# Two MLP groups of a fused attention and MLP layer go from 16 to 18 paired rows in seven products; one maximum for two tiles, a mask by GpSimd, and a few moved instructions

## The chip, the cores and the metric

The kernel runs on one core of a Trainium2 chip. The core has five engines that run their own instruction streams: TensorE (PE in the profile, with its weight loads listed apart as PEld), VectorE (DVE), ScalarE (ACT), GpSimd (POOL) and SyncE (SP), which here only issues DMAs. Semaphores order them. The metric is the device time of one execution in microseconds, the median over runs.

## The reference

One transformer layer over 2048 positions of width 576, in bfloat16, without learned norms:

```python
x = A_x
h = x + A(_layernorm(x))          # 32 heads of 18; key s-2w for w in 0..7, softmax over 8 logits, then @ wo
h2 = h + B(_layernorm(h))         # gelu(y @ w1 + b1) @ w2 + b2, inner width 4608
```

In the attention each position looks at itself and at seven earlier positions, two apart; positions before the start are masked with -1e9.

## The kernel before

**Tiles and groups.** The 2048 positions are 16 tiles of 128 rows, `x3[:, j, :]`. Row p of tile j is position 16p + j, so the keys "two apart" of one tile lie in the tiles of the same parity, or in the same tiles one row up; only row 0 has masked keys. `ATT_ORDER` is 14, 12, ..., 0, 15, 13, ..., 1, and `GROUPS` are its eight pairs, from (14, 12) to (3, 1). A first stage (to about 65 us) makes Q, K and V for all tiles. Then comes a loop over the eight groups (L1031); its turn for group k is called step k here. `x_all` and `q_all` are the SBUF homes of x and of q, one row of 576 bfloat16 for each tile; rows whose tile is through are used again for other things.

**What a step does.** Step k computes the MLP of group k while VectorE prepares the attention of groups k+1 and k+2. On TensorE a step is: the first MLP product with `w1` (`mlp1`, the tile `pm`), the attention's output product with `wo` for the two tiles c, d of group k+1 (`wo_visit`, `pw`), then the second MLP product with `w2` (`po`). The order of all engines' instructions is written out by hand: lists of hooks (`m1`, `x["hc"]`, `x["h"]`, `x["6"]`, `x["7"]`, `x["in"]`, `x["exp"]`, `x["4"]`, `x["3"]`) are called between the parts of TensorE's work, and each engine runs its share in that order.

**The attention chain.** In step k VectorE makes, for c and d, the weighted sums over V (`pv_sum`: L401, L407, L408, at the start of the step). `send_o` stores the result o to a DRAM scratch `td`, and `read_o` reads it back with a transposing DMA into `oT`, the weights of the `wo` product. After that, still on VectorE: products of q and k for tile e of group k+2 (`att_qk_a`, `att_qk_b`), with a memset that masks row 0 (L364); later the same for f. `att_max` takes the maximum over the 8 keys and subtracts it (L368, L369), ScalarE takes one exponential for both tiles (`exps`), `att_den` divides. The product for f waits by hand for the `pow` on GpSimd that makes the second 1/std of the next norm (`root`, L346).

**The second MLP product in seven products.** `w2` has 36 row blocks; two neighbours make a pair, so there are `NM = 18` pairs. For a pair, two tiles and two halves of the 576 columns make a 2x2 by 2x2 block product. It can be done as eight products, or as seven with sums (Winograd's form): `w2_sums` prepares sums of weights once (four of them, `t_slot`), and `h_sums` in each step prepares four sums of the hidden activations (`s_slot`), which VectorE writes. Groups 0 and 1 use the plain form (`mlp2`); groups 2 to 5 use seven products over the first 16 pairs and the plain form for the last two (`plain`, hooks "11", "12", "21", "22"); groups 6 and 7 (`FULL`) use seven products over all 18. `mlp2_fast` lists the order; "b", "d" and "f" are copies on ScalarE of one PSUM bank to another (L774), which the next product adds to. In step 7 the second product (2) stands after the sixth.

**Homes of the sums.** The four sums of pairs 0 to 11 lie in `kv_ring0` and in `h_all` in place; those of pairs 12 to 15 in rows of `q_all` (15, 13, 11; in step 2 also `x_all` 10 and 8). The weight sums of pairs 16 and 17 are made in step 6 into `kv_ring1`, which is free by then.

**DMA order.** All loads and stores of SP stand in one hand-written queue. The x rows of the odd tiles are loaded a second time (`reload_x`): those of group k+3 late in step k, for k from 1 to 4 (at hook "in" in steps 3 and 4, at "3" in step 2). GpSimd issues the adding DMAs (`out_sum`, `accumulate_h`). The four quarters of `wo` are loaded in the first stage after visits 5 (two), 8 and 11.

Of the kernel before, what the change touches and what calls it, by code (L numbers as in the profile page):

```python
# [17 lines left out]
def kernel(  # L18
# [336 lines left out]

    ADDS = ((0, 0, 9), (0, 0, 4), (0, 0, 2), (0, 0, 1))

    def att_qk_b(j, i, skip=0):
        side[j] = i
        out = logit_of([j])[:, 0]  # L360
        att_qk_add(j, ADDS[skip:])
        nc.vector.tensor_tensor(out=out, in0=prod[:, :, 0:H], in1=prod[:, :, 8 * H:9 * H], op=ALU.add)
        if j // 2 + 1 < W:
            nc.vector.memset(out[0:1, j // 2 + 1:W, :], -1e9)  # L364

    def att_max(js):
        n, sl, lg = len(js), sides(js), logit_of(js)
# [248 lines left out]
    def t_slot(t, m0, m1):  # L616
        if t == 2:
            return w2_block(0, 1, m0, m1).bitcast(F16)
        i = (0, 1, None, 2)[t]
        if m0 >= 16:  # L620
            return ring_blocks(1, (2 * i + m0 - 16) * HALF, m1 - m0, HALF)
        if i == 2 and m0 < 16:
            return ring_blocks(0, RING_T + m0 * HALF, m1 - m0, HALF)
        part = 0 if m1 <= 8 else 1 if m1 <= 12 else 2
        rows, j0 = ((x_all, (1, 9, 13)[part]), (q_all, (4, 12, 0)[part]))[i]
        m = m0 - (0, 8, 12)[part]
        j = j0 + 2 * (m // 2)
# [6 lines left out]
    step_of = [0]  # L634
    RING_T = 3 * SR * P

    def s_slot(t, m0, m1):
        if t == 2:
            return h_block(0, 1, m0, m1)
        i = (0, 1, None, 2)[t]  # L640
        if m0 < SR:
            return ring_blocks(0, (i * SR + m0) * P, m1 - m0, P)
        if not ring1_free[0]:
            rows, j = ((q_all, 15), (x_all, 10), (x_all, 8))[i] if step_of[0] == 2 else (q_all, 15 - 2 * i)
            return rows[:, j, (m0 - SR) * P:(m1 - SR) * P].bitcast(F16).rearrange("p (m c) -> p m c", c=P)
        return ring_blocks(1, 6 * HALF + (i * (NM - SR) + m0 - SR) * P, m1 - m0, P)

    def h_block(odd, i, m0, m1):
        return h_all[:, 2 * m0 + odd:2 * m1:2, i * P:(i + 1) * P].bitcast(F16)
# [53 lines left out]
        return ap.rearrange("p (g c) -> p g c", g=2)  # L703

    def mlp2_fast(g, rows, tags, wo, hooks):
        last, summed = wo is None, rows < NM
# [24 lines left out]

        def out1():
            if summed:
                add(o1[:, HALF:D], bank[5], o1[:, 0:HALF])
                add(o1[:, 0:HALF], b, o1[:, 0:HALF])
                out_sum(j1)
                return
            add(o1[:, 0:HALF], b, rest[:, 0])
            add(o1[:, HALF:D], bank[5], rest[:, 1])
            nc.sync.dma_start(out=out3[:, j1, :], in_=o1)  # L740

        def do_rest():
# [16 lines left out]
        if rows < NM:  # L759
            steps = ["wo", "hc", (1, all_), "b", "h", "e", (7, lo), (2, all_), (6, all_), "6", "7", "d", "11", (7, hi), "rest", "in",  # L760
                      (5, all_), "f", "exp", (4, all_), "21", "22", "o1", "4", (3, all_), "12", "o0", "3"]
        elif not last:
            steps = ["wo", "hc", (1, all_), "b", "h", "e", (7, lo), (6, all_), "6", "d", "7", (2, all_), (7, hi), "rest", "in",
                     (5, all_), "f", (4, all_), "o1", "4", (3, all_), "o0"]
        else:
            steps = ["e", (1, lo), (7, lo), (1, hi), "b", "h", (7, hi), "rest", (6, all_), "d", (2, all_), "lo",
                     (5, all_), "f", (4, all_), "o1", (3, all_), "o0"]
        for step in steps:
            if isinstance(step, tuple):
                product(step[0], bank[step[0]], *step[1])  # L770
            elif step == "f" and last:
                add(f, bank[5], x_of(j0)[:, HALF:D])
            elif step in seed:
                nc.scalar.copy(out=bank[seed[step][1]], in_=bank[seed[step][0]])  # L774
            else:
                call([does[step]] if step in does else hooks.get(step, ()))
# [22 lines left out]
    with tc.manual_schedule(engines={ENG.PE, ENG.Activation, ENG.DVE, ENG.SP, ENG.Pool}):  # L799
# [129 lines left out]
            ln2_ins(c, d)  # L929

        loads = {}
        for v, fns in ((2, [(load_w1, 0)]), (3, [(load_w1, 1)]), (4, [(load_w1, 2)]), (5, [(load_wo, [0, 1])]), (8, [(load_wo, [2])]),
                       (11, [(load_wo, [3])]), (14, [(load_w1, 4)]), (18, [(load_w1, 5), (load_w2, 0)]), (19, [(load_w2, 1)]),
                       (20, [(load_w2, 2)]), (21, [(load_w2, 3)]), (22, [(load_w2, 4)])):
            loads[v] = [c_(*fn) for fn in fns]
        after = {
# [9 lines left out]
                c_(store_halo, A[1]), c_(store_halo, A[0], slice(1, 2))],  # L946
            9: [c_(ln1_act, 9, 0)],
            10: [c_(att_pv, A[0]), c_(ln1_act, 9, 1), c_(in_x, 1), c_(halo, A[1], 1)],
            11: [c_(out_x, 2), c_(halo, A[0], 2)],
            12: [c_(ln1_act, 10, 0)],  # L950
            13: [c_(ln1_act, 10, 1), c_(in_x, 2), c_(out_x, 3), c_(load_w1, 3), c_(store_halo, A[2]), c_(store_halo, A[3])],
            14: [c_(att_pv, A[1]), c_(in_x, 3), c_(load, b2_bc, B_b2.partition_broadcast(P))],
# [71 lines left out]
        def wo_visit(*duos, fill=False):  # L1024
            visit([wo_duo(j, tag) for j, tag in duos], (lambda: [ahead[0]() for _ in range(2)]) if fill else None)

        FULL = (6, 7)
        p, q, r, s = "ABDC"

        gelu_table()  # L1030
        for k, g in enumerate(GROUPS):  # L1031
# [36 lines left out]
            step_of[0] = k  # L1068
            x = {n: [] for n in ("hc", "h", "6", "7", "in", "exp", "4", "3")}
            if 2 < k < 7:  # L1070
                m1[0] += [c_(pv_sum, c), c_(send_o, c), c_(pv_sum, d), c_(read_o, c), c_(send_o, d), c_(read_o, d)]
            if k < 6:
                m1[1] = m1.get(1, []) + [c_(att_qk_a, e), c_(att_qk_b, e, 0)]
                x["hc"] += [c_(halo, e, 1)]
                m1.setdefault(3, [])
                if k == 2:
                    m1[0] += [c_(pv_sum, d), c_(send_o, d), c_(read_o, d)]
# [4 lines left out]
                x["h"] += [c_(h_sums, 0, SR, (1, 3) if k == 2 else (3,)), c_(h_sums, SR, 16)]  # L1082
                x["7"] += [c_(att_max, [e]), c_(att_qk_one, f, 1), c_(att_max, [f])]
                x["exp"] += [c_(exps, e, f)]
                x["4"] += [c_(att_den, e, f)]
            else:
                if k == 6:
                    ring1_free[0] = True
                    m1[1].append(c_(w2_sums, 16, NM))
                m1[3] = m1.get(3, []) + [c_(h_sums, 0, SR)]  # L1090
                if k == 7:
                    mid[3] = {1: [c_(h_sums, SR, 16)]}
                    x["h"] += [c_(h_sums, 16, NM)]
            if k + 3 < len(GROUPS):
# [55 lines left out]
```

## Time and profile before

| | us |
|---|---|
| median of 3 runs (lowest, highest) | 358.68 (357.99, 359.8) |
| the profiled execution, its own time | 358.89 |
| its span, first to last instruction | 357.1 |
| TensorE busy in the span | 352.1 (99%) |
| VectorE busy | 298.1 (83%) |
| ScalarE busy | 235.5 (66%) |
| GpSimd busy | 48.4 (14%) |
| granted TensorE clock | 1.000 |

The page gives busy time by engine, the span in 40 slices, the DMA queues, the chain of work that ended last, and the costliest groups of instructions. Beside it stand answers of the trace: the timeline of one engine (start, duration, engine, line, operation, out<-in, count, and in brackets idle time before it with what ended it), the chain in order of time, and the instructions of one tile with the time from a DMA's issue to its landing. Line numbers are those of the kernel before. Step 3 runs from 177 to 213 us, step 4 to 249, step 5 to 285, step 6 to 320, step 7 to the end.

### The profile page before, as it was taken

What the parts mean: (1) busy time and instruction counts of PE and PEld (TensorE: products, weight loads), DVE (VectorE), ACT (ScalarE), POOL (GpSimd) and SP (SyncE); (2) the same over time, 40 slices, a digit from 0 to 9 for tenths busy, and PEclk for the clock granted to TensorE, in tenths of its full rate; (3) what the DMA queues carried; (4) which work ended last, traced back from release to release, by engine and by line L of the source; (5) the groups of instructions that cost most, each with busy time, mean ns of one, the idle gap of its engine ahead of it and who ended that gap; (6) DMA issues with size and microseconds to landing.
All of it is one profiled execution on the core that took longest, in us unless ns stands there. A gap on an engine that the chain in (4) does not pass through costs nothing.

```text
span 357.1 us, 11588 instructions
## 1 busy us (share of the span) xinstructions
PE 352.1 (99%) x4945; PEld 290.2 (81%) x4945; DVE 298.1 (83%) x428; ACT 235.5 (66%) x524; POOL 48.4 (14%) x63
## 2 busy tenths in 40 slices
PE   8999999999999999999999999999999999999996
PEld 4777878998788877887788778877887788778874
DVE  4999999999988999999999989998999897520431
ACT  4889756996647783668566856695669566706620
POOL 2241004000212010201200220022002200210000
PEclk9999999999999999999999999999999999999999
DMA  7996599953837573742653445345555353262001
GB/s 242 330 317 165 156 262 286 388 200 81 213 71 113 172 230 70 139 72 61 93 97 84 114 106 81 86 107 109 85 86 103 63 88 50 59 126 41 4 1 33
DMA packets 63492, 46.29 MB, mean 130 GB/s; under 512 B 32192, under 2 KB 61760, under 8 KB 63440
## 3 DMA queue, kind: packets, MB, share of 16 engines
q1 hardware_dynamic: 59472, 41.50, 43.7%
q0 software_dynamic: 3744, 3.84, 9.8%
q8 instruction: 38, 0.62, 0.7%
q10 hardware_dynamic: 224, 0.22, 0.2%
q14 instruction: 14, 0.11, 0.1%
HBM read 23.38 MB, written 12.42 MB: 100 GB/s over the span
## 4 chain that ended last, share of the span: by engine, by line
PE 92%; DMA 3%; DVE 2%; ACT 1%; issue 0%; POOL 0%; SPq 0%; ACTq 0%; POOLq 0%
PE pm L222 39%; PE po L687 25%; PE pq L222 12%; PE po L597 10%; PE pw L222 5%; DMA x_all<-in_A_x_dram 1%; DMA wq_sb<-in_A_wqkv_dram 1%; ACT h_all L578 1%; DVE ln_stats L148 1%; DVE q_all L844 0%; DVE kv_ring L667 0%; DVE ln_mv L149 0%; POOL ln_rstd L161 0%; ACT q_all L314 0%; SPq L104 0%
## 5 line engine op out<-in xcount | busy, mean ns | idle before, releaser
L222 PE MATMUL pm<-hnT,w_sb 64*128 64x256 bf16 x2304 | 142.9, 269 | 0.0
L578 ACT ACTIVATE h_all<-pm,b_sb 128x256 f16<-128x256 f32 (+1 forms) x288 | 108.4, 495 | 50.9 <-PE pm L222 50.3
L222 PEld LDWEIGHTS <-w_sb 64*128 64x128 bf16 x2304 | 113.3, 94 | 13.4 <-issue 1.7
L222 PE MATMUL pq<-wq_sb,xnT 64*128 64x288 bf16 x720 | 54.7, 283 | 0.7 <-ACT q_all L314 0.3
L687 PEld LDWEIGHTS <-h_all 128*128 128x128 f16 x464 | 44.8, 98 | 12.9 <-issue 1.4
L222 PEld LDWEIGHTS <-xnT 64*128 64x128 bf16 x864 | 42.0, 94 | 11.7 <-issue 0.8
L353 DVE TENSOR_TENSOR prod<-prod 128x2304 bf16<-128x2304 bf16 (+1 forms) x64 | 44.2, 691 | 2.1
L401 DVE TENSOR_TENSOR prod<-kv_ring,probs 128x4608 bf16<-128x4608 bf16 x16 | 40.9, 2558 | 1.7 <-DMA kv_ring<-kv_dram 1.2
L344 DVE TENSOR_TENSOR prod<-kv_ring,q_all 128x4608 bf16<-128x4608 bf16 x16 | 40.9, 2556 | 1.6 <-POOL ln_rstd L492 1.3
L222 PE MATMUL pm<-hnT,w1h_sb 64*128 64x256 bf16 x288 | 39.5, 269 | 0.0
L407 DVE TENSOR_TENSOR prod<-prod 128x2304 bf16<-128x2304 bf16 (+1 forms) x32 | 33.9, 1058 | 1.1
L597 PEld LDWEIGHTS <-h_all 128*128 128x128 bf16 x288 | 27.8, 98 | 8.0 <-issue 1.2
L687 PE MATMUL po<-w2a_sb,h_all 128*128 128x288 bf16 (+1 forms) x252 | 34.0, 286 | 0.0
L687 PEld LDWEIGHTS <-kv_ring 128*128 128x128 f16 x252 | 24.7, 98 | 6.2
L597 PE MATMUL po<-w2a_sb,h_all 128*128 128x288 bf16 x224 | 28.6, 286 | 0.0
L787 POOL DMA_DIRECT2D x_all<-o_sb x12 | 10.7, 889 | 126.0 <-PE pw L222 72.6
L222 PE MATMUL pq<-wqh_sb,xnT 64*128 64x288 bf16 x144 | 27.4, 283 | 0.0
L492 POOL TENSOR_TENSOR ln_rstd<-ln_var,mhalf 128x1 f32<-128x1 f32 x13 | 10.6, 818 | 77.1 <-ACT ln_var L491 50.1
L667 DVE TENSOR_TENSOR kv_ring<-h_all 128x1536 f16<-128x1536 f16 (+3 forms) x9 | 6.8, 754 | 15.9 <-ACT h_all L578 15.9
L222 PE MATMUL pw<-wo_sb,oT 64*128 64x288 bf16 x256 | 19.5, 283 | 0.0
L161 POOL TENSOR_TENSOR ln_rstd<-ln_veps,mhalf 128x1 f32<-128x1 f32 (+2 forms) x14 | 13.1, 948 | 45.2 <-DVE ln_nmean L481 27.5
L687 PE MATMUL po<-w2b_sb,h_all 128*128 128x288 bf16 (+1 forms) x112 | 18.8, 286 | 0.1
(121 smaller groups left out, 410.9 us busy)
## 6 DMA issues: line engine op xcount, KB each, us to landing
w_sb<-in_B_w_dram SPq DMA_DIRECT2D x6, 768.0 KB, 6.6
kv_ring<-kv_dram SPq DMA_DIRECT2D x28, 144.0 KB, 2.4
kv_dram<-kv_ring SPq DMA_DIRECT2D x13, 288.0 KB, 3.2
w2a_sb<-in_B_w_dram SPq DMA_DIRECT2D x3, 1008.0 KB, 10.0
x_all<-in_B_b_dram SPq DMA_DIRECT2D x15, 144.0 KB, 4.2
td<-q_all SPq DMA_DIRECT2D x14, 144.0 KB, 1.8
td<-hn SPq DMA_DIRECT2D x14, 144.0 KB, 1.8
x_all<-h POOLq DMA_DIRECT2D x14, 144.0 KB, 4.7
```

The source lines that it names most:

```text
L161: nc.gpsimd.tensor_tensor(out=rstd[:], in0=veps[:], in1=mhalf[:].to_broadcast([P, n]), op=ALU.pow)
L222: last = nc.tensor.matmul(duo["g"][r ^ swap][i], lhsT=lhsT, rhs=rhs, start=(swap == 0 and i == 0 and kt == 0), stop=(swap == 1 and kt == K ...
L344: ins = nc.vector.tensor_tensor(out=prod[:], in0=k_ring[j % 2], in1=q_all[:, j, :].unsqueeze(1) .to_broadcast([P, W, D]), op=ALU.mult).ins
L353: nc.vector.tensor_tensor(out=prod[:, :, o * H:o * H + n], in0=prod[:, :, a * H:a * H + n], in1=prod[:, :, c * H:c * H + n], op=ALU.add)
L401: nc.vector.tensor_tensor(out=prod[:].rearrange("p w (d h) -> p w d h", h=H), in0=v_ring[j % 2].rearrange("p w (d h) -> p w d h", h=H), in ...
L407: nc.vector.tensor_tensor(out=prod[:, 0:n, :], in0=prod[:, 0:n, :], in1=prod[:, n:2 * n, :], op=ALU.add)
L492: ins = nc.gpsimd.tensor_tensor(out=rstd[:], in0=var[:], in1=mhalf[:], op=ALU.pow).ins
L578: pace[0] = nc.scalar.activation(out=hT(grp)[:, f, 0:N], in_=ps[:, r, i * N:(i + 1) * N], func=ACT.Gelu_apprx_tanh, bias=b1_sb[:, f:f + 1] ...
L597: nc.tensor.matmul(banks[half], lhsT=hT(grp)[:, f, i * P:(i + 1) * P], rhs=w2_rows(f)[:, half * HALF:(half + 1) * HALF], start=(f == 0), s ...
L667: nc.vector.tensor_tensor(out=s_slot(t, m0, m1), in0=a, in1=b, op=alu)
L687: nc.tensor.matmul(bank, lhsT=l, rhs=r, start=start, stop=stop, skip_group_check=True)
L787: nc.gpsimd.dma_start(out=x_of(j), in_=o_of.pop(j), accum_op=ALU.add)
```

## The change

- `FULL` becomes groups 4 to 7: in steps 4 and 5 all 18 pairs go through the seven products, the plain matmuls go. `summed`, which decides how the outputs are written, is tied to the group instead (groups 6 and 7 differ as before).
- VectorE makes the four activation sums of pairs 16 and 17 in steps 4 and 5. In step 4 it also makes two of the four weight sums of these pairs, in step 3 the other two; step 6 no longer makes them. They lie in `q_all` 15, 13 and 11.
- The homes of pairs 12 to 17 are listed by step (`homes`); in steps 4 and 5 the second sum lies in a tile of tag `hnT`, the buffer of the normed and transposed h (`new_top`). As written, the third home of these steps takes the fourth sum of pairs 12 to 15, then over the same 512 columns the first and the fourth sum of pairs 16 and 17, before the products read them; the values of that part of the output follow from it.
- In steps 4 and 5 the mask of tile e is written by GpSimd between its two `pow`, and the maximum of e and f is taken in one instruction after f's product (one subtraction too). The mask of f stays on VectorE.
- `reload_x` of group k+1 stands in steps 4 and 5 between `send_o(c)` and `read_o(c)`; that of group 7 stays in step 4 at "in"; those in steps 2 and 3 go.
- Step 7: the second product's first six pairs stand between the two parts of the seventh product's last six pairs.
- `wo`: one quarter after visit 5, one after visit 8, and two after visit 11's `out_x`, ahead of the halo read.

```diff
-    def att_qk_b(j, i, skip=0):
+    def att_mask(j, engine=nc.vector):
+        if j // 2 + 1 < W:
+            engine.memset(logit_of([j])[0:1, 0, j // 2 + 1:W, :], -1e9)
+
+    def att_qk_b(j, i, skip=0, mask=True):
...
         if m0 >= 16:
-            return ring_blocks(1, (2 * i + m0 - 16) * HALF, m1 - m0, HALF)
+            return q_all[:, 15 - 2 * i, (m0 - 16) * HALF:(m1 - 16) * HALF].bitcast(F16).rearrange("p (m c) -> p m c", c=HALF)
...
+    homes = {2: ((q_all, 15), (x_all, 10), (x_all, 8)), 3: ((q_all, 11), (x_all, 10), (x_all, 8)),
+             4: ((q_all, 9), (x_all, 4), (x_all, 6)), 5: ((q_all, 9), (q_all, 5), (q_all, 7))}
...
+            if step_of[0] in FULL and t == 1:
+                rows, c = top[0][:].rearrange("p k c -> p (k c)"), 0
+            else:
+                rows, j = homes[step_of[0]][2 if m0 >= 16 else i]
+                rows, c = rows[:, j, :], (16 - SR - i) * P if m0 >= 16 else 0
+            return rows[:, (m0 - SR) * P - c:(m1 - SR) * P - c].bitcast(F16).rearrange("p (m c) -> p m c", c=P)
...
+    def new_top():
+        top[0] = sb.tile([P, KT, 2 * P], BF16, tag="hnT", name="hnT")
...
-            steps = ["e", (1, lo), (7, lo), (1, hi), "b", "h", (7, hi), "rest", (6, all_), "d", (2, all_), "lo",
+            steps = ["e", (1, lo), (7, lo), (1, hi), "b", "h", (7, (SR, 16)), (2, (0, 6)), (7, (16, rows)), "rest", (6, all_), "d",
+                     (2, (6, rows)), "lo",
...
-            11: [c_(out_x, 2), c_(halo, A[0], 2)],
+            11: [c_(out_x, 2), c_(load_wo, [2, 3]), c_(halo, A[0], 2)],
...
-        FULL = (6, 7)
+        FULL = (4, 5, 6, 7)
...
-                m1[0] += [c_(pv_sum, c), c_(send_o, c), c_(pv_sum, d), c_(read_o, c), c_(send_o, d), c_(read_o, d)]
+                m1[0] += [c_(pv_sum, c), c_(send_o, c)] + [c_(reload_x, GROUPS[k + 1])] * (k in (4, 5)) + [c_(pv_sum, d), c_(read_o, c), c_(send_o, d), c_(read_o, d)]
...
-                m1[1] = m1.get(1, []) + [c_(att_qk_a, e), c_(att_qk_b, e, 0)]
-                x["hc"] += [c_(halo, e, 1)]
+                m1[1] = m1.get(1, []) + [c_(att_qk_a, e), c_(att_qk_b, e, 0, 0, k < 4)]
+                x["hc"] += [c_(halo, e, 1)] + [c_(att_mask, e, nc.gpsimd)] * (k >= 4)
...
+                if k in FULL:
+                    x["h"] += [new_top, c_(h_sums, SR, 16), c_(h_sums, 16, NM)] + [c_(w2_sums, 16, NM, (2, 3))] * (k == FULL[0])
...
-                x["7"] += [c_(att_max, [e]), c_(att_qk_one, f, 1), c_(att_max, [f])]
+                first = [e] if k < 4 else []
+                x["7"] += [c_(att_max, first)] * len(first) + [c_(att_qk_one, f, 1), c_(att_max, [f] if first else (e, f))]
+                if k == 3:
+                    x["exp"] += [c_(w2_sums, 16, NM, (0, 1))]
...
-                    m1[1].append(c_(w2_sums, 16, NM))
...
-            if k + 3 < len(GROUPS):
-                x["3" if k == 2 else "in"] += [c_(reload_x, GROUPS[k + 3])]
+            if k == 4:
+                x["in"] += [c_(reload_x, GROUPS[7])]
```

More of the change, by code (lines that the diff above doesn't have):

```diff
@@ L362, in att_qk_b @@
         nc.vector.tensor_tensor(out=out, in0=prod[:, :, 0:H], in1=prod[:, :, 8 * H:9 * H], op=ALU.add)
-        if j // 2 + 1 < W:
-            nc.vector.memset(out[0:1, j // 2 + 1:W, :], -1e9)
+        if mask:
+            att_mask(j)
     def att_max(js):
@@ L633 @@
     ring1_free = [False]
-    step_of = [0]
+    step_of, top = [0], [None]
+    homes = {2: ((q_all, 15), (x_all, 10), (x_all, 8)), 3: ((q_all, 11), (x_all, 10), (x_all, 8)),
+             4: ((q_all, 9), (x_all, 4), (x_all, 6)), 5: ((q_all, 9), (q_all, 5), (q_all, 7))}
     RING_T = 3 * SR * P
@@ L643, in s_slot @@
         if not ring1_free[0]:
-            rows, j = ((q_all, 15), (x_all, 10), (x_all, 8))[i] if step_of[0] == 2 else (q_all, 15 - 2 * i)
-            return rows[:, j, (m0 - SR) * P:(m1 - SR) * P].bitcast(F16).rearrange("p (m c) -> p m c", c=P)
-        return ring_blocks(1, 6 * HALF + (i * (NM - SR) + m0 - SR) * P, m1 - m0, P)
+            if step_of[0] in FULL and t == 1:
[4 more added lines that the diff above has]
+            return rows[:, (m0 - SR) * P - c:(m1 - SR) * P - c].bitcast(F16).rearrange("p (m c) -> p m c", c=P)
+        return ring_blocks(1, (i * (NM - SR) + m0 - SR) * P, m1 - m0, P)
+    def new_top():
+        top[0] = sb.tile([P, KT, 2 * P], BF16, tag="hnT", name="hnT")
     def h_block(odd, i, m0, m1):
@@ L705, in mlp2_fast @@
     def mlp2_fast(g, rows, tags, wo, hooks):
-        last, summed = wo is None, rows < NM
+        last, summed = wo is None, g not in GROUPS[6:]
         q, p, r, s = tags
@@ L758, in mlp2_fast @@
         }
-        if rows < NM:
+        if summed:
             steps = ["wo", "hc", (1, all_), "b", "h", "e", (7, lo), (2, all_), (6, all_), "6", "7", "d", "11", (7, hi), "rest", "in",
@@ L931 @@
         loads = {}
-        for v, fns in ((2, [(load_w1, 0)]), (3, [(load_w1, 1)]), (4, [(load_w1, 2)]), (5, [(load_wo, [0, 1])]), (8, [(load_wo, [2])]),
-                       (11, [(load_wo, [3])]), (14, [(load_w1, 4)]), (18, [(load_w1, 5), (load_w2, 0)]), (19, [(load_w2, 1)]),
+        for v, fns in ((2, [(load_w1, 0)]), (3, [(load_w1, 1)]), (4, [(load_w1, 2)]), (5, [(load_wo, [0])]), (8, [(load_wo, [1])]),
+                       (14, [(load_w1, 4)]), (18, [(load_w1, 5), (load_w2, 0)]), (19, [(load_w2, 1)]),
                        (20, [(load_w2, 2)]), (21, [(load_w2, 3)]), (22, [(load_w2, 4)])):
@@ L1081 @@
                 x["hc"] += [c_(h_sums, 0, SR, (2,) if k == 2 else (1,))]
-                x["h"] += [c_(h_sums, 0, SR, (1, 3) if k == 2 else (3,)), c_(h_sums, SR, 16)]
-                x["7"] += [c_(att_max, [e]), c_(att_qk_one, f, 1), c_(att_max, [f])]
+                x["h"] += [c_(h_sums, 0, SR, (1, 3) if k == 2 else (3,))]
+                if k in FULL:
+                    x["h"] += [new_top, c_(h_sums, SR, 16), c_(h_sums, 16, NM)] + [c_(w2_sums, 16, NM, (2, 3))] * (k == FULL[0])
+                else:
+                    x["h"] += [c_(h_sums, SR, 16)]
+                first = [e] if k < 4 else []
+                x["7"] += [c_(att_max, first)] * len(first) + [c_(att_qk_one, f, 1), c_(att_max, [f] if first else (e, f))]
+                if k == 3:
+                    x["exp"] += [c_(w2_sums, 16, NM, (0, 1))]
                 x["exp"] += [c_(exps, e, f)]
```

## The prediction

> **What bounds the kernel now.** I read the page first (busy time, the slices), then the chain in order of time, then TensorE's timeline for every gap in it, then VectorE's and SP's timelines of steps 3 to 6 for how much room they leave.
>
> The page's busy rows, then pieces of the chain in order of time:
>
> ```profile
> PE 352.1 (99%) x4945; PEld 290.2 (81%) x4945; DVE 298.1 (83%) x428; ACT 235.5 (66%) x524; POOL 48.4 (14%) x63
> ...
> 195.09 2.31 PE pw L222 x36
> 197.40 15.79 PE po L687 x128
> 213.19 17.79 PE pm L222 x324
> 230.97 2.21 PE pw L222 x36
> 233.18 15.79 PE po L687 x128
> ...
> 268.96 15.79 PE po L687 x128
> ...
> 304.75 15.54 PE po L687 x126
> ```
>
> From 65 us to the end of step 6 the chain is TensorE work without a gap, at one speed: every first product takes 17.79, every `wo` visit 2.2. So time goes only with TensorE's instructions, unless something else comes late. The second product in its old form takes 15.79 us for 128 matmuls (steps 2 to 5), in the form that steps 4 and 5 are to get 15.54 us for 126 (step 6). The one visible wait is 2.31 instead of 2.21 in step 3, where the transposed o of the second tile came late.
>
> The timeline of step 7 shows the other stall (matmuls, ScalarE's copy "b", and the weight load that waits for VectorE's sums):
>
> ```profile
> 341.94 0.97 PE L687 MATMUL po<-w2b_sb,h_all 128*128 128x288 f16 x4
> ...
> 341.95 0.38 ACT L774 COPY po<-po 128x288 f32<-128x288 f32 x1 [0.37 <-PE po L687]
> ...
> 342.49 0.11 PEld L687 LDWEIGHTS <-h_all 128*128 128x128 f16 x2 [0.45 <-DVE h_all L667]
> ...
> 342.75 2.12 PE L687 MATMUL po<-q_all,kv_ring 128*128 128x288 f16 x16
> ```
>
> One matmul comes each 0.1225 us (15.79/128 is 0.123). Four from 341.94 should end at 342.43; the sixth product starts at 342.75, so 0.32 us is lost waiting for pairs 16 and 17.
>
> Not TensorE but the closest behind it is VectorE: in steps 3 to 5 it idles about 1 us of 35.8.
>
> **The change, part by part.** The sum is made against the profiled execution, 358.89 us (span 357.1, and 1.79 around it), which lies 0.21 above the median 358.68.
>
> *Seven products over 18 pairs.* 7 x 18 = 126 matmuls for 7 x 16 + 16 = 128, in two steps. By the two rows 15.79 - 15.54 = 0.25 each: -0.50 us, all on the path. The seventh product's last part now has six matmuls and nothing plain beside it to cover ScalarE's copy "d". In step 4 that copy started 0.20 after the sixth product's last matmul and took 0.38; six matmuls are 0.735, so 0.15 is left, less a wake-up (0.06 from VectorE's end to the weight load at 342.49). Cost nothing; if the copy were behind something else on ScalarE, that delay comes out in full.
>
> *VectorE's share.* Prices from its own rows: a weight sum of two pairs, 128x576, 0.47; four activation sums of 128x256 in a row 0.94 (step 7: 341.62 to 342.5); a maximum over one tile 0.59 and its subtraction 0.42, for two tiles 1.04 (as the sum over both, L395) and 0.69 (L397). Step 3: +0.93, of which its 0.62 idle before the output adds takes two thirds: VectorE enters step 4 0.3 late. Step 4: mask gone -0.1, activation sums +0.94, weight sums +0.93, first maximum -1.0, and the wait of 0.44 for `pow` before f's product is filled: f's product starts 0.63 late. The common maximum at the end adds 0.7, the wait of 0.57 behind it goes: VectorE leaves step 4 about 0.8 late. Step 5, without weight sums: about 0.9 late. None of this is on the path by itself. Nearest needs: sums of pairs 16 and 17 are ready at 239.4 in step 4 and read from 241.7; the exponential moves 1.4 us, before ScalarE's next activations at 251.9.
>
> *What is queued behind it.* o of tile d is stored and read back 0.8 to 0.9 us later in steps 5 and 6, while TensorE asks for it 0.25 and 0.5 earlier. This is the thin place. SP's issue and, from the tile's own answers, the time to landing (for the issues at 262.4 and 298.5):
>
> ```profile
> 262.43 1.21 SPq L439 DMA_TRANSPOSE oT<-td  x1
> DMA to landing us min/median/max: 4.6/4.6/4.6
> ...
> 298.51 1.21 SPq L439 DMA_TRANSPOSE oT<-td  x1
> DMA to landing us min/median/max: 2.8/2.8/2.8
> ...
> 267.21 0.65 PE L222 MATMUL pw<-wo_sb,oT 64*128 64x288 bf16 x8
> ```
>
> Of the 11 landings that the trace holds eight took 2.8 to 3.2, one 3.7, two 4.6 and 4.7; the median is 3.0. In step 5 the transpose would issue at 263.25 and land at 266.1 to 266.3 for a need at 266.97: 0.7 to 0.9 of room, but a loss of 0.9 if the 4.6 repeats. In step 6: issue 299.4, landing 302.25 to 302.4, need 302.99 - 0.49 = 302.5: 0.1 to 0.25 of room. I take 3.0, the median, so 0; ends 0 and +1.5.
>
> *`hnT` as a home.* The transposing loads of the next normed h must wait until the sixth product has read the second sum. In step 4 that product ends at 241.2; the loads issued at 242.09. No cost; if it slipped, they land at 246.2 and the next step starts at 248.65, so 2.4 us is the cover.
>
> *GpSimd's mask.* Memsets there took 0.10 to 0.20 (the 128x128 identity). It stands between two `pow`, with 1.4 us of room in step 4 (236.65 to 238.01), and its reader is the maximum, 8 us later. Upper end: a GpSimd instruction that starts beside a long VectorE product is held until it ends:
>
> ```profile
> 24.94 2.55 DVE L344 TENSOR_TENSOR prod<-kv_ring,q_all 128x4608 bf16<-128x4608 bf16 x1
> 25.05 3.00 POOL L161 TENSOR_TENSOR ln_rstd<-ln_veps,mhalf 128x2 f32<-128x2 f32 x1 [1.47 <-DVE ln_nmr L170]
> ```
>
> Beside the mask stand sums of at most 0.95, so 0.1 to 0.95 in a room of 1.4: 0. The second `pow` would then stand beside sums of 0.45 at most; it lengthens the way to `hnT` inside its 2.4 us.
>
> *Step 7.* The six matmuls between fill the wait, but they go into the bank that ScalarE's copy "b" is still reading, to 342.33. So they start at about 342.4 rather than 342.19; then six and the two last of product 7, and the sixth product is 6 x 0.1225 later for the matmuls done ahead: (342.39 + 8 x 0.1225) - 6 x 0.1225 = 342.64 against 342.75. -0.1 us; ends -0.32 (no wait for the copy) and 0.
>
> *Reloads and `wo`.* The reload puts two issues (1.04 us) before the transposed read of c's o, which has some 5 us until its use, and 288 KB on the queues 2.5 to 4 us before d's store; the issues that steps 2 and 3 lose (176.84, 208.90) stood ahead of nothing that TensorE waited for. SP idles from 39.3 to 43.07 where the two `wo` quarters go (about 1.9 us of issues), and the transposes after them move ahead by the 0.9 us that a quarter took there. A weight load waited 0.24 for one of these transposes (50.11), so -0.1 to 0; I take 0.
>
> Sum: 358.89 - 0.50 - 0.10 = 358.29 us; on the scale of the median, 0.21 lower, 358.1 us, 0.17% faster. A measurement of this kernel can tell about 0.5% (1.8 us) from no change.
>
> **The rivals.**
>
> *The gain is taken by o.* One of the two late transposes takes 4.6 rather than 3.0. For: two or three of the 11 landings. Against: eight leave room, or lose less than 0.05. Worked out: step 5 alone +0.9, step 6 alone 299.4 + 4.6 - 302.5 = +1.5: 358.1 + 0.9 to 1.5 = 359.0 to 359.6. It decides from a landing of 3.7 in step 5 or 3.1 in step 6. Within 0.5%.
>
> *Slower: the reload in front of d's store.* Step 2 has that picture, a reload issued just ahead of a store of o (SP's timeline, and below it the landing of that store from the scratch tile's answer):
>
> ```profile
> 145.38 1.42 SPq L462 DMA_DIRECT2D x_all<-in_A_x_dram  x2
> ...
> 147.38 1.00 SPq L204 DMA_DIRECT2D td<-q_all  x1
> DMA to landing us min/median/max: 4.1/4.1/4.1
> ```
>
> 4.1 rather than 1.7, and the transpose behind it 3.7 rather than 2.8: 3.3 us. In step 5, less 0.9 of room, that is 2.4 us of standing TensorE; in step 4, with 1.6 of room, 1.7, which gives step 5 the same back; then step 6's 0.1 or more. About 358.1 + 2.4 = 360.5, 0.5% slower. Against: there the store came 0.6 us after the reloads' issue ended and beside adding DMAs of GpSimd; here it comes 2.5 to 4 us after, and GpSimd's DMAs of the step are through by 218 and 254. It decides from 2.4 us of total wait. [...]
>
> *Faster by more than 0.5%.* It would need 1.8 us; all TensorE gaps after 65 us that the change touches come to 0.50 + 0.32 + 0.1 + 0.1 = 1.0. Only the spread of the runs speaks for it. 357.7 at best, 357.3 with the run's spread.
>
> **How the numbers follow.** A landing of 3.7 or more came 3 times in 11, and either step can have it: no loss 8/11 x 8/11 = 0.53. Forecast 0.50; gain taken by o 0.33; slower by the reload or another late chain 0.12; faster 0.05. The first two are within 0.5%: same 0.83, slower 0.12, faster 0.05. The range goes from the forecast less the step 7 and transposed-load ends (0.4) and half the runs' spread below (0.3) to the upper end of the second case with a little of its spread: 357.4 to 359.9.
>
> **What would show it.** Right: `po` at 15.54 in steps 4, 5 and 6, step 7's gap under 0.25, `wo` visits at 2.2. Wrong: a `wo` visit of step 5 or 6 over 2.3 that ends on `oT`, a reload landing after 4 us, or idle time before a first product in step 5 or 6 (`hnT`); a copy "d" that holds the fifth product. VectorE should leave step 5 0.9 us later relative to TensorE's old times.

## The result and the profile after

The changed kernel took 357.78 us (median of 18 runs, 357.32 to 358.57), the kernel before in the same series 358.34 (18 runs, 357.83 to 359.8): ratio 0.998 with a 95% interval from 0.9972 to 0.9988, or 0.56 us less (0.43 to 1.0). That is within 0.5%, the case forecast, and 0.3 below the predicted 358.1. The profiled execution took 357.48 us, its span 355.7.

The page's busy rows of the changed kernel (share of the span, instructions after the x):

```profile
PE 350.9 (99%) x4941; PEld 289.5 (81%) x4941; DVE 299.1 (84%) x430; ACT 235.1 (66%) x524; POOL 48.3 (14%) x65
```

Four matmuls fewer, as counted, and 1.2 us less of TensorE; VectorE has two instructions and 1.0 us more. The chain in order of time (start, duration, engine, tile, line, instructions):

```profile
194.37 2.21 PE pw L222 x36
...
232.36 15.54 PE po L700 x126
247.90 17.79 PE pm L222 x324
265.69 2.21 PE pw L222 x36
267.89 15.54 PE po L700 x126
...
301.22 2.21 PE pw L222 x36
303.43 15.54 PE po L700 x126
...
336.76 4.27 PE po L700 x34
341.07 11.45 PE po L700 x92
```

The second product takes 15.54 in steps 4, 5 and 6, every `wo` visit 2.21, and the chain is TensorE without a gap to step 7. Step 7's second product stands in two rows. What lies between them, in TensorE's timeline:

```profile
340.62 0.41 PE L700 MATMUL po<-w2b_sb,h_all 128*128 128x288 f16 x2
341.07 0.90 PE L700 MATMUL po<-w2a_sb,h_all 128*128 128x288 bf16 x6
...
342.05 2.37 PE L700 MATMUL po<-q_all,kv_ring 128*128 128x288 f16 x18
```

and the copy "b" in ScalarE's timeline:

```profile
340.63 0.38 ACT L788 COPY po<-po 128x288 f32<-128x288 f32 x1 [0.37 <-PE po L700]
```

The six matmuls moved forward start when the copy has ended (341.01), as forecast: two matmuls from 340.62 take 0.245, so 0.2 us is lost ahead of 341.07. The sixth product starts 5.36 us after the first product; before it was 342.75 - 338.01 = 4.74 with six matmuls fewer ahead (0.735). So 0.115 is won. The `po` rows of steps 4, 5 and 7 and the visit of step 3 (2.21, before 2.31) are all that changed between the first `pm` and the end: 287.62 us from that `pm` to the start of the last `po` matmul, before 288.34. The difference of 0.72 is 0.50 + 0.115 + 0.10.

The places named as thin, in SP's timeline (the transposed reads of the second tile's o in steps 5 and 6):

```profile
262.42 2.05 SPq L443 DMA_TRANSPOSE oT<-td  x1
...
297.36 1.22 SPq L443 DMA_TRANSPOSE oT<-td  x1
```

They landed 3.15 and 2.82 us after their issue, at 265.57 and 300.18. The rows of TensorE that need them:

```profile
266.14 0.65 PE L222 MATMUL pw<-wo_sb,oT 64*128 64x288 bf16 x8
...
301.67 0.65 PE L222 MATMUL pw<-wo_sb,oT 64*128 64x288 bf16 x8
```

So the room was 0.57 in step 5 and 1.49 in step 6. The first `pm` starts at 64.59 instead of 65.32; among the profiles that follow it started between 64.50 and 65.25 with no order in it, so starts and ends are compared from each profile's own first `pm`.

### The profile page after: what moved, and what is told of

Read it like the earlier page. It is cut to its first block, busy times and chain, and to the rows that moved or that the text cites. A ratio compares the mean times of both kernels' runs of the same rounds, so it can differ in the third digit from the quotient of the medians.

```text
span 355.7 us, 11595 instructions
## 1 busy us (share of the span) xinstructions
PE 350.9 (99%) x4941; PEld 289.5 (81%) x4941; DVE 299.1 (84%) x430; ACT 235.1 (66%) x524; POOL 48.3 (14%) x65
## 4 chain that ended last, share of the span: by engine, by line
PE 81%; DVE 14%; DMA 2%; issue 1%; ACT 0%; POOL 0%; ACTq 0%; SPq 0%; DVEq 0%
PE pm L222 40%; PE po L700 26%; PE po L601 10%; PE pw L222 4%; DVE ln_stats L148 3%; DMA x_all<-in_A_x_dram 2%; DVE prod L353 2%; DVE prod L344 2%; DVE prod L405 1%; DVE prod L411 1%; DVE ln_mv L149 1%; PE pq L222 0%; DVE q_all L858 0%; DVE h L471 0%; DVE peak L372 0%
## 5 line engine op out<-in xcount | busy, mean ns | idle before, releaser
L700 PEld LDWEIGHTS <-h_all 128*128 128x128 f16 x448 | 43.3, 98 | 12.4 <-issue 1.6
L788 ACT COPY po<-po 128x288 f32<-128x288 f32 x17 | 6.5, 385 | 19.9 <-PE po L700 19.9
```

Of the source, the lines that this page charges most:

```text
L700: nc.tensor.matmul(bank, lhsT=l, rhs=r, start=start, stop=stop, skip_group_check=True)
```

## The experiments

Each edit is shown against the changed kernel; a ratio is to the kernel before on the same chip, with its 95% interval. The third home is written over as in the changed kernel, except with 16 pairs and with the edit to the homes.

**The matmul count: 16 pairs again in steps 4 and 5.**

```diff
-            rows = NM if k in FULL else 16
+            rows = NM if k in (6, 7) else 16
...
-                    x["h"] += [new_top, c_(h_sums, SR, 16), c_(h_sums, 16, NM)] + [c_(w2_sums, 16, NM, (2, 3))] * (k == FULL[0])
+                    x["h"] += [new_top, c_(h_sums, SR, 16)]
...
+                    m1[1].append(c_(w2_sums, 16, NM, (2, 3)))
```

> The changed kernel with steps 4 and 5 back at 16 pairs in seven products and two in the plain form; the common maximum, GpSimd's mask, the moved reloads, the wo loads and step 7's order stay, and two of the four weight sums of pairs 16 and 17 go back to step 6. Theory (matmul count): the second product of steps 4 and 5 takes 15.79 us instead of 15.54, so the kernel is 0.5 us slower than the changed one and about 0.1 to 0.2 us faster than the one before (ratio 0.9995). Rival (the gain came from VectorE's lighter end of the step or from the moved DMAs): it stays at the changed kernel's ratio of 0.998.

358.28 us (11 runs; before 358.47), ratio 0.9991 [0.9982, 1.0]. The chain:

```profile
232.87 15.79 PE po L700 x128
...
268.65 15.79 PE po L700 x128
```

288.11 us from the first `pm` to the start of the last `po` matmul, 0.49 over the changed kernel: the count is worth its 0.50, and everything else of the change together little.

**Step 7 and the loads of `wo`: both as before.**

```diff
-            steps = ["e", (1, lo), (7, lo), (1, hi), "b", "h", (7, (SR, 16)), (2, (0, 6)), (7, (16, rows)), "rest", (6, all_), "d",
-                     (2, (6, rows)), "lo",
+            steps = ["e", (1, lo), (7, lo), (1, hi), "b", "h", (7, hi), "rest", (6, all_), "d", (2, all_), "lo",
...
-(5, [(load_wo, [0])]), (8, [(load_wo, [1])]),
+(5, [(load_wo, [0, 1])]), (8, [(load_wo, [2])]), (11, [(load_wo, [3])]),
...
-            11: [c_(out_x, 2), c_(load_wo, [2, 3]), c_(halo, A[0], 2)],
+            11: [c_(out_x, 2), c_(halo, A[0], 2)],
```

> The changed kernel with step 7's order and the loads of wo as before: groups 4 and 5 with all that belongs to them alone. Theory: 0.1 us slower than the changed kernel, 0.5 us faster than before (ratio 0.9986); the sixth product of step 7 starts 4.74 us after the first again. Rival (the moved wo loads gave the 0.7 us by which the first MLP product started sooner in the changed kernel's profile): no faster than before.

357.91 us (11 runs), ratio 0.9982 [0.9973, 0.999]. The sixth product starts 4.74 after the first again, so the 0.115 is step 7's order. The first `pm` starts at 64.57: the moved loads gave the first stage nothing that a profile shows. The visit of step 3 waited some 0.2 here; in eight of the twelve experiments it took 2.3 or more, or stood broken by a wait, and in the others 2.21. It comes and goes from profile to profile, so nothing here ties the 0.10 of the comparison above to a part of the change.

**Step 7 with the copy covered.** On top of the edit to the homes below:

```diff
-            steps = ["e", (1, lo), (7, lo), (1, hi), "b", "h", (7, (SR, 16)), (2, (0, 6)), (7, (16, rows)), "rest", (6, all_), "d",
+            steps = ["e", (1, lo), (7, (0, 10)), (1, hi), "b", "h", (7, (10, 16)), (2, (0, 6)), (7, (16, rows)), "rest", (6, all_), "d",
```

> As the run with separate homes, and in step 7 two matmuls of the seventh product's first part stand behind the first product, so that six instead of four lie between it and the second product's first six. Theory (the six matmuls wait for ScalarE's copy of the first bank): 0.2 us of that wait is covered, the sixth product starts 0.2 us sooner after the step's first matmul of the second product than in the changed kernel (5.36 there, 5.15 here), provided that the first product's last pair, which comes 0.25 us earlier, does not wait for its activations; 0.2 us off the time. Rival (they wait for VectorE's sums, or for a fixed cost of changing banks): 5.36 again.

357.45 us (6 runs), ratio 0.9969 [0.9958, 0.9981]: the fastest of all versions run here. TensorE's timeline:

```profile
340.68 0.41 PE L700 MATMUL po<-w2b_sb,h_all 128*128 128x288 f16 x2
340.92 0.90 PE L700 MATMUL po<-w2a_sb,h_all 128*128 128x288 bf16 x6
...
341.90 2.37 PE L700 MATMUL po<-q_all,kv_ring 128*128 128x288 f16 x18
```

Copy "b" ran from 340.44 to 340.82, and the six follow without a gap: the sixth product starts 5.15 after the first, 0.21 sooner than in the changed kernel. With that step 7's wait of 0.32 is gone.

**The cover of copy "d".** Four of the six last matmuls of the seventh product move ahead of the copy, so that two are left behind it:

```diff
-            steps = ["wo", "hc", (1, all_), "b", "h", "e", (7, lo), (2, all_), (6, all_), "6", "7", "d", "11", (7, hi), "rest", "in",
+            steps = ["wo", "hc", (1, all_), "b", "h", "e", (7, lo), (2, all_), *[(7, (SR, 16))] * (rows == NM), (6, all_), "6", "7", "d", "11", (7, (16, rows) if rows == NM else hi), "rest", "in",
```

> The changed kernel; in steps 4 and 5 four of the six last matmuls of the seventh product stand before the sixth product, so only two are left to cover ScalarE's copy d behind it. Theory (the fifth product waits for that copy: 0.20 us to its start, 0.38 for it, some 0.06 to wake): 0.64 less 2 x 0.1225 is 0.40 us of wait in each of the two steps, the second product takes 15.9 us there, the kernel about 0.8 us more. Rival (the copy does not hold the fifth product up): 15.54.

358.70 us in one run (358.74 in one run of the kernel before beside it). The chain breaks in both steps:

```profile
232.83 8.70 PE po L700 x70
241.98 6.78 PE po L700 x54
...
268.75 8.70 PE po L700 x70
277.90 6.78 PE po L700 x54
```

241.98 - (232.83 + 8.70) = 0.45 of waiting, the same in step 5, where 0.40 was worked out. So in the changed kernel six matmuls cover the copy, and by little.

**The homes: the fourth sums of pairs 12 to 15 keep their own place.**

```diff
-                rows, j = homes[step_of[0]][2 if m0 >= 16 else i]
+                rows, j = homes[step_of[0]][1 if m0 >= 16 else i]
```

> The changed kernel with the sums of pairs 16 and 17 in the second home of steps 4 and 5 instead of the third, so that the fourth sum of pairs 12 to 15 is not written over; instructions and order are the same. Theory: the shared home orders only instructions of one engine that stand in order anyhow; time as the changed kernel, ratio 0.998, second product 15.54 in steps 4 to 6. Rival (the changed kernel waits, or saves a wait, on the shared home): a wait before the fifth or the third product, 0.1 us or more a step.

357.73 us (10 runs), ratio 0.9979 [0.997, 0.9988], and 287.62 us between the marks, to the hundredth what the changed kernel has. The gain does not come from writing over the third home; this edit keeps the sums apart at no cost in time.

**VectorE made late: one or two extra additions at the start of step 5** (on scratch that nothing reads):

```diff
+        def late_dve(n):
+            for _ in range(n):
+                nc.vector.tensor_tensor(out=prod[:, 0:4, :], in0=prod[:, 0:4, :], in1=prod[:, 4:8, :], op=ALU.add)
...
-                m1[0] += [c_(pv_sum, c), c_(send_o, c)] + ...
+                m1[0] += [c_(late_dve, n)] * (k == 5) + [c_(pv_sum, c), c_(send_o, c)] + ...
```

> The changed kernel with one more VectorE instruction of 1.37 us (half of the key products, added in place, written over right after) at the start of step 5. Theory (VectorE is off the path while the second tile's transposed o is in time): o of that tile comes 1.37 later; the changed kernel's profile left 0.57 us there, so TensorE waits 0.8 us in the wo visit of step 5 (2.2 becomes 3.0) if the transpose takes its 2.8 to 3.2; nothing is lost elsewhere. Rival (the room that I gave in the prediction, none to 0.9 with VectorE 0.8 late): 0.5 to 1.4 us. Rival (VectorE binds through another wait, the sums): a wait in the second product.

> The same with two such instructions, 2.74 us. Theory: 2.74 less 0.57, so 2.2 us of wait in the wo visit of step 5, and the whole kernel 2.2 us slower than the changed one; 1.37 more than with one instruction. Rival (something else binds VectorE): less than 1.37 between the two.

360.55 and 362.00 us, one run each (the kernel before beside them 358.74, one run). TensorE's timeline with one addition:

```profile
269.21 0.66 PE L222 MATMUL pw<-wo_sb,oT 64*128 64x288 bf16 x8 [1.87 <-DMA oT<-td]
```

and with two:

```profile
269.28 1.14 PE L222 MATMUL pw<-wo_sb,oT 64*128 64x288 bf16 x8 [2.57 <-DMA oT<-td]
```

TensorE stood where the theory put it, and nowhere else in steps 4 to 6; the sizes were wrong. With one addition 0.8 was expected and 1.87 came: the second store of o (64 columns, issued at 262.75) was followed by its read only at 266.32, 3.6 later, where 1.6 to 1.7 is usual. With two, 2.2 was expected and 2.57 came; VectorE itself lost 1.05 there, waiting for a halo read (`kv_ring<-kv_dram`). So the way from VectorE to TensorE through o is the thin place, and how much a delay costs depends on what its DMAs meet. What the slow store met is seen in the next experiment; the second case has one more price, told in the last section.

**The reload directly ahead of d's store.**

```diff
-                m1[0] += [c_(pv_sum, c), c_(send_o, c)] + [c_(reload_x, GROUPS[k + 1])] * (k in (4, 5)) + [c_(pv_sum, d), c_(read_o, c), c_(send_o, d), c_(read_o, d)]
+                m1[0] += [c_(pv_sum, c), c_(send_o, c)] + [c_(pv_sum, d), c_(read_o, c)] + [c_(reload_x, GROUPS[k + 1])] * (k in (4, 5)) + [c_(send_o, d), c_(read_o, d)]
```

> The changed kernel with the two reloads of x in steps 4 and 5 directly ahead of the store of the second tile's o, the picture of step 2. Rival of the prediction (a reload beside a store of o makes the store land after 4.1 instead of 1.7 us and the transpose after 3.7 instead of 2.8): o comes up to 3.3 us later, TensorE waits some 2.5 us in step 5 and 1.5 in step 4, the kernel 2.5 us slower or more. Theory (the 4.1 of step 2 came from the adding DMAs of GpSimd): the store lands within 0.5 us of its usual 1.8, the wo visits lengthen by 0.5 us at most.

362.63 us in one run, 3.9 over the kernel before. SP's timeline in step 5:

```profile
262.35 1.00 SPq L466 DMA_DIRECT2D x_all<-in_A_x_dram  x2
263.44 0.38 SPq L204 DMA_DIRECT2D td<-q_all  x1
263.88 0.43 SPq L205 DMA_DIRECT2D td<-q_all  x1
268.50 1.21 SPq L443 DMA_TRANSPOSE oT<-td  x1
```

and TensorE's, steps 4 and 5:

```profile
232.73 0.66 PE L222 MATMUL pw<-wo_sb,oT 64*128 64x288 bf16 x8 [1.22 <-DMA oT<-td]
...
271.31 0.66 PE L222 MATMUL pw<-wo_sb,oT 64*128 64x288 bf16 x8 [2.87 <-DMA oT<-td]
```

Here the theory (at most 0.5 us) fell, and the waits had the size that the rival gave (1.5 and 2.5). The store's large part landed after 2.7 and 2.6 us (1.75 and 2.1 in the changed kernel); the read behind the small part was issued 4.3 and 4.6 after it (1.6 and 1.7 there). The read itself landed in 2.9 and 2.8 (3.0 and 3.15 there). So the large part of the store was 0.9 and 0.5 later than in the changed kernel, the small part, by the issue of the read behind it, 2.7 and 2.9; the read, issued some 5 us after the reload's issue had ended (224.94 and 263.35), was not later at all.

The small part met something that SP's rows do not list. The DMA view of step 5, first from 265.9 to 267.2, then from 267.2 to 268.5 (queue, packets, MB, share of the 16 DMA engines):

```profile
q8 instruction: 1, 0.02, 4.5%
...
q1 hardware_dynamic: 7, 0.00, 1.1%
```

By 265.9 all but seven packets of SP's loads and stores had run. Then one packet of 16 KB ran alone, on the queue that the page calls instruction, and took 0.9 us (4.5% of 16 engines over 1.3 us); the last seven ran when it was over. Step 4 has the same order (the packet at 227.4, the last seven at 228.6), and so has the run with one late addition (the packet at 264.1, the last nine of the store at 265.1 to 265.4). That this packet held the store up is read from the order; no run tests it. The page has 38 such packets, as that of the changed kernel has:

```profile
q8 instruction: 38, 0.62, 0.8%
```

So the reload's own share may be only the 0.9 and 0.5 of the large part: with it ahead, the small part was still under way when the packet came. In the changed kernel the packets came at 226.5 and 263.0, after the reads behind the small stores had been issued (225.89 and 262.42). There the reload's issue ended 2.4 us ahead of the store in step 4 (221.48 to 223.90) and 1.9 in step 5 (258.19 to 260.11), its last part had landed by then (223.57 and 260.08), and no visit waits.

**The mask back on VectorE.**

```diff
-                m1[1] = m1.get(1, []) + [c_(att_qk_a, e), c_(att_qk_b, e, 0, 0, k < 4)]
-                x["hc"] += [c_(halo, e, 1)] + [c_(att_mask, e, nc.gpsimd)] * (k >= 4)
+                m1[1] = m1.get(1, []) + [c_(att_qk_a, e), c_(att_qk_b, e, 0)]
+                x["hc"] += [c_(halo, e, 1)]
```

> The changed kernel, with the mask of tile e written by VectorE again in steps 4 and 5; nothing else differs. Theory (an instruction of VectorE costs its neighbours the time from start to start, not its own busy time): from the last sum of the logits to the first activation sum 0.60 to 0.67 us instead of 0.34, as in the kernel before. In step 4 VectorE then waits for the wo product anyway (0.23 in the changed kernel), so the product for f starts at most 0.05 later there, counted from the first pm; in step 5, where it does not wait, VectorE leaves the step about 0.3 later. TensorE has no gap by it: the second product stays at 15.54 in steps 4 to 6, and the time at that of the changed kernel, within 0.2 us. Rival (the prediction's price): the mask is worth its busy time, 0.1 to 0.2, so that the distances are 0.44 to 0.54. Either way the mask by GpSimd is worth nothing in time.

357.77 us (10 runs; before 358.52), ratio 0.9988 [0.9978, 0.9998]: the time of the changed kernel. VectorE's timeline with the mask back:

```profile
265.92 0.42 DVE L366 TENSOR_TENSOR logits<-prod 128x256 f32<-128x256 bf16 x1
266.44 0.22 DVE L360 MEMSET logits<- 1x192 f32 x1
266.59 0.88 DVE L680 TENSOR_TENSOR kv_ring<-h_all 128x1536 f16<-128x1536 f16 x1
```

and in the changed kernel:

```profile
265.58 0.43 DVE L366 TENSOR_TENSOR logits<-prod 128x256 f32<-128x256 bf16 x1
265.92 0.95 DVE L680 TENSOR_TENSOR kv_ring<-h_all 128x1536 f16<-128x1536 f16 x1
```

From start to start 0.67 against 0.34: the memset of 0.22 costs 0.33 (0.26 in step 4), and VectorE left step 5 0.41 later, of which TensorE had lost 0.15 before, in step 3; about 0.3 was expected. No wait came of it.

**The maxima apart again: in both steps, in step 5 alone, in step 4 alone.**

```diff
-                first = [e] if k < 4 else []
+                first = [e]                       # both
+                first = [e] if k != 4 else []     # step 5 alone
+                first = [e] if k != 5 else []     # step 4 alone
```

> The changed kernel, with the maxima and subtractions of e and f taken apart again in steps 4 and 5 (e's ahead of the product for f); the mask stays with GpSimd. Theory: e's maximum and subtraction (0.58 and 0.42) move ahead of f's product, which starts about 1.05 later in step 4 (near 239.4 where the changed kernel has 238.3); behind it stands 1.0 instead of 1.73, so VectorE leaves step 4 0.3 later and step 5 0.6 to 0.7 later. The store of the second tile's o in step 5 is 0.3 later, inside the room of 0.57 that the changed kernel showed, and 0.6 to 0.7 later in step 6, inside 1.49: no wo visit over 2.3, the second product at 15.54, the time that of the changed kernel within 0.2 us. Rival (the prediction's picture, room of 0.1 to 0.25 in step 6): a wait on oT of 0.4 to 0.6 in step 6, and the time up by as much.

> The changed kernel, with the maxima of e and f apart again in step 5 alone. With both steps so, the store of the second tile's o in step 6 came 0.92 later than in the changed kernel, its transposed read took 4.3 to land instead of 2.8, and the wo visit of step 6 waited 0.6 to 0.8. Theory (lateness adds up over the steps, and step 6 is where it is paid): from step 5 alone VectorE leaves about 0.35 later, or 0.8 if its second output add waits for TensorE again as it did with both steps apart. The read of o in step 6 is then 0.35 to 0.8 later, counted from the first pm; with a landing of 2.8 that leaves room (1.49 in the changed kernel) and no wait, and the time is that of the changed kernel; with a landing of 4.2 or more the visit waits 0.2 to 0.7 and the time is 0.2 to 0.7 higher. Rival (the cost lies in step 4, not here): no lateness in step 6 at all.

> The changed kernel, with the maxima of e and f apart again in step 4 alone. Theory: VectorE leaves step 4 0.3 later, has no wait in step 5 ahead of the adds to h but about 0.4 for the pow that the common maximum left none of, and is back in time by the end of step 5: the read of o in step 5 is 0.3 later inside a room of 0.57 (no wait over 0.1 unless its landing takes over 3.5), that in step 6 at most 0.3 later, and the time is that of the changed kernel within 0.2 us. Rival (the cost of both steps apart came from step 4): a time 0.4 to 0.6 higher.

| maxima apart in | us (10 runs; 18 in the last row) | ratio | read of d's o in step 6, after the first `pm` | its landing |
|---|---|---|---|---|
| steps 4 and 5 | 358.41 | 0.9998 [0.9989, 1.0008] | 233.69 | 4.27 |
| step 5 | 357.75 | 0.9983 [0.9974, 0.9993] | 232.96 | 2.81 |
| step 4 | 357.72 | 0.9985 [0.9974, 0.9996] | 233.11 | 2.73 |
| none (changed kernel) | 357.78 | 0.998 [0.9972, 0.9988] | 232.77 | 2.82 |

Both together give the whole gain back; either alone costs nothing. TensorE's timeline with both, step 6:

```profile
301.49 0.65 PE L222 MATMUL pw<-wo_sb,oT 64*128 64x288 bf16 x8
...
302.87 0.66 PE L222 MATMUL pw<-wo_sb,oT 64*128 64x288 bf16 x8 [0.61 <-DMA oT<-td]
```

The second eight start 1.38 after the first instead of 0.61 (301.06 to 301.67 in the changed kernel): 0.77 us of standing TensorE, in one profile; that the medians differ by nearly as much (358.41 against 357.77 for the kernel with the mask back, run beside it) suggests that it is the rule there. Two things had to meet: the read 0.92 later (0.76 against its need, since TensorE had itself lost 0.16 in step 3), and a landing of 4.27. Late alone, with 2.8, it would have kept 0.7 of the 1.49. Step 4 alone gives 0.34 of lateness (the expectation had it made up for by the end of step 5; it was not), step 5 alone 0.19; another 0.46 with both is VectorE waiting for TensorE between the two output adds of step 5:

```profile
283.24 0.46 DVE L731 TENSOR_TENSOR o_sb<-po,o_sb 128x288 f32<-128x288 f32 x1 [0.46 <-PE po L700]
```

Why that add waits here and runs straight behind the first in the changed kernel was not settled. Beside the slow landing SP's rows show no load, but the DMA view has an instruction packet again (from 300.5 to 301.5, then from 301.5 to 302.9):

```profile
q8 instruction: 1, 0.02, 6.0%
...
q1 hardware_dynamic: 2, 0.00, 0.2%
```

It started at 300.8, 2.26 us after the read's issue, and the read's last two packets ran when it was over. In the changed kernel it came 2.5 after the issue, when the read's last packets were through. The expectation for both together had the lateness (0.6 to 0.7) and the room, and missed the time; what it called the prediction's picture, a wait on `oT` in step 6, is what came.

## Why the prediction was right, point by point

- **126 matmuls for 128, -0.50.** Right to the hundredth, shown by undoing it.
- **Step 7, -0.10.** Right: 0.115, through the copy "b", which the run with the copy covered confirms from the other side.
- **Copy "d" at nothing, 0.15 left.** Right. In step 4 the copy ran from 240.59 to 240.97 and the fifth product started at 241.12, 0.15 behind it. With two matmuls of cover the wait was 0.45.
- **VectorE's share.** The mis-sized term. Against the kernel before, each from its own first `pm`, VectorE entered step 4 0.04 late (0.3 predicted), started f's product there 0.28 late (0.63), left step 4 0.42 late (0.8) and step 5 0.08 early (0.9 late). Three errors show: step 3's two weight sums fit into the wait before the output adds almost whole; the two in step 4 took 0.74 from start to start (237.57 to 238.31), not 0.93; and the mask was worth 0.26 and 0.33, not 0.1. The largest was one of bookkeeping: its own prices give 0.8 - 0.1 + 0.94 - 1.0 - 0.44 + 0.7 = 0.9 for step 5, with the wait of 0.44 ahead of f's product taken off and that of 0.49 ahead of the output adds left in. With both taken off they give 0.4.
- **o of the second tile.** No loss, as taken, with other rooms: 0.57 in step 5 (0.7 to 0.9 predicted) and 1.49 in step 6 (0.1 to 0.25), the latter because VectorE was not late, and because a wait of 0.38 for a halo read in step 6 was gone.
- **The landing as a draw.** The chance of 3 in 11 per step was the wrong picture. Of the eleven profiles without added delay or a moved reload, the two in which step 5's read was issued 197.0 and 197.1 after the first `pm` (16 pairs, and the kernel before) had it land in 4.65; the nine that issued it from 197.3 to 198.3 in 2.8 to 3.7. Being later cost nothing: the change moved the read from 197.1 to 197.8. In these eleven the landing goes with the distance from the read's issue to the start of the next instruction packet: 2.8 and 2.9 us where it was 0.0 to 0.2, 3.15 to 3.3 at 0.4 to 0.5, 3.4 to 3.65 at 0.9 to 1.2, 4.65 at 2.5. In step 6 the packet came 2.3 to 2.9 after the issue in thirteen of the fourteen profiles, and these reads landed in 2.7 to 2.9; the fourteenth is the one with 4.27. This order was found in the profiles, not tested by itself.
- **The slower rival.** With the reload directly ahead of the store its two waits came near (1.7 and 2.4 worked out, some 1.4 and 3.0 measured from start to start), but not its sum. It had step 4's wait give step 5 the same back, for 2.4 in all; both were paid, 4.4, since VectorE's adds to h wait for the visit and VectorE left step 4, counted from the first `pm`, 1.8 later than in the changed kernel (0.4 of it from step 3). What made the store so late was, by the traces, not the reload alone. Where the change puts the reload, none of it happens.
- **The gain taken by o.** Did not come, but was near: the kernel with both maxima apart is that rival, with 0.8 lost where 0.9 to 1.5 was worked out.
- **The common maximum.** The prediction's ledger has both of its parts, 1.0 off ahead of f's product and 0.7 more at the end of the step, but gave the 0.3 that it saves (1.73 for both tiles, against twice 1.0) no worth in time. Without it in both steps the change loses its gain. In either step alone it moves no time.
- **The mask by GpSimd and the moved loads of `wo`.** Nothing, as taken. The mask took 0.20 and 0.25 on GpSimd beside VectorE's sums, not the 0.95 of the upper end. The sums that VectorE started with it (235.77 and 271.30) took 0.42, as those of the same size right after them, and the next ones followed 0.34 later.

The sum was 0.60 below the kernel before; 0.72 stood in the profiles and 0.56 in the medians. That 357.78 lies under 358.1 is the scale: the kernel before was 358.34 in this series and 358.68 in the three runs that the prediction had.

## What to carry to other kernels

TensorE's chain had no gap from the first `pm` to step 7: two matmuls taken out of a step were worth their 0.25 us, and what VectorE got more (1.0 us in all) was worth nothing as long as its waits and the room ahead of TensorE took it up; 1.37 more at the start of step 5, against 0.57 of room, cost 1.87. In a kernel of this kind keep that ledger step by step, each step with its own waits, and by times from start to start. Parts of a change that measure zero alone can hold each other up, as the two maxima did here (358.41 us with both apart, 357.75 and 357.72 with one): test them together and apart before one is called useless. A small store that another engine waits for should not stand right behind a large load in the same queue: with the reload right ahead it was still under way when an instruction packet came, and TensorE waited 1.22 and 2.87 us; with the reload's issue over 2.4 and 1.9 us ahead of the store no visit waited. When a DMA lands late and its own queue shows no reason, look at the other queues of the DMA view.

## What was not expected of the hardware

- Packets of the instruction queue, 16 KB each, went with the late DMAs here. With one coming while it was under way, the 64-column store of the second tile's o (16 KB) had its read issued 3.6 to 4.6 us after it, where 1.6 to 1.7 is usual in steps 4 to 6; with a reload ahead (4.3 and 4.6), the larger store between the two landed after 2.6 to 2.7. Of the reads of o whose landing the traces hold none took more than 3.3 us in any profile without such a packet starting between its issue and its landing.
- The price of a wait was not only its length. After the wait of 2.57 us (two extra additions) TensorE's granted clock was 0.50 from 269.2 to 270.4 and 0.56 on the mean from there to 272.4 (0.50 from 268.75 to 272.1, 1.00 from 272.2), and the 26 matmuls left of that visit took 3.15 us; after the longer wait of 2.87 (the reload ahead of the store) the clock stayed at 1.00 and the same 26 took 1.77. The chain, with two additions:

```profile
269.28 3.15 PE pw L222 x26
```

  and with the reload ahead:

```profile
271.31 1.77 PE pw L222 x26
```

  The clock fell when TensorE had stood 2.0 us (from 266.7), and only one of the two times; what set it off was not shown.
- With the mask back on VectorE, its memset of one row cost the neighbours 0.26 us in step 4 and 0.33 in step 5, for 0.17 and 0.22 of its own.
